# Another explicit order for the first task list of a gated attention and state-space kernel

## The chip, the cores and the metric

The kernel runs on one core of one Trainium2 chip. The metric is the device time of one execution in microseconds (us). Durations of single instructions come from a profile of one execution. A core has these engines, each with a queue of its own that is run in order: TensorE (PE; its weight loads are shown apart, as PEld), VectorE (DVE), ScalarE (ACT), GpSimd (POOL) and SyncE (SP, which here only issues transfers). They wait for each other through semaphores.

## The reference

With x of 2048 rows and 640 columns:

```python
g = sigmoid((x * gate_w).sum(-1, keepdims=True))
a = attention(x, wqkv) @ wo        # 32 heads of 20; each row looks at itself and 7 rows before it, 2 apart
b = conv(x, K) + x * Dskip         # per column, over the rows, through an FFT of length 4096
return g * a + (1 - g) * b
```

The convolution's kernel K has 2048 taps for each of the 640 columns and is made from parameters: with dt = exp(log_dt), K[d, l] is the real part of the sum over 192 states n of C[d, n] * dt * B[d, n] * exp(dt * A[d, n] * l), all complex.

## The kernel before

The work is written down as *tasks*. `Plan.add` records a name, the engines that could run it, nominal durations, a function that emits its instructions, and what it depends on. A task that may run on ScalarE or on VectorE (an eviction out of PSUM, a scaling) has both letters, "A" and "D". `Plan.order` then reads a list of numbers: number k is the k-th task recorded, and a letter behind it (97A, 99D) says which engine runs it. `Plan.emit` emits the tasks in that order and ties each instruction to the one before it on its engine, so that the list alone sets the order of every engine's queue, SyncE's and GpSimd's transfers included. There are two lists. SEQ1 has 1090 tasks and covers all up to the transforms; SEQ2 has 237, covers the spectral products, the inverse transform and the output, and starts when SEQ1's work is done.

The tasks of SEQ1, by name, with the lines that their instructions have in the profile:

- Parameters (L564 to L616): 74 tasks, most on VectorE and ScalarE, turn the parameter arrays into twelve pieces, stored to DRAM (sp0 to sp11). The lin tasks (L597, L599) are those of them that may run on either engine.
- turn0 to 9 with tev0 to 9 (L200, L470): x transposed. late0 to 59 (L291): the projections to q, k and v, five products each, into the PSUM tile tb; lev0 to 59 evict them (L470 on ScalarE, L472 on VectorE). lst (L317) stores v.
- gate to gst: the gate g.
- Attention, for eight blocks sc of 256 rows: prod (L351, VectorE) and lg (L357, TensorE) make the logits; max, neg, exp, sum and at the softmax; ast and asb (L396, L401, SyncE) send it to DRAM and fetch it back spread; vc (L345, GpSimd) fetches v; pv (L420, VectorE) weighs it; gat (L426) sums; oT (L470, L472) evicts; wo (L444) projects; ga (L453 on ScalarE, L455 on VectorE) scales by g and evicts; gaS (L464) stores.
- K, in ten chunks c of 64 columns: L (L721, SyncE) fetches parameters; arg (L748, TensorE) makes arguments, two in flight in the PSUM tile ar; act (L760 sine, L762 exponential, ScalarE) evaluates them, 18 to a chunk; pq (L783 to L785, VectorE) multiplies, three to a chunk; kmm (L801, TensorE) sums, four to a chunk, each of 64 weight loads and 64 products; fin (L1215, VectorE) gathers.
- After chunks 4 and 9, half of K is expanded: shift, move, near, own and other build tile X (L832 to L847); xst (L873 to L876) stores it to DRAM and xld (L881) loads it back as kc.
- First transforms (L1232), each evicted with a task of its own (L470, L472): f1 (ten, of kc's first half), fu (twenty, of x itself) and fk (ten, of kc's second half). rows (L946) fetch x for fu.

What sets the end of SEQ1 is written by hand only in so far as the list is: the second half's X, store, load, and the ten fk with their evictions are its last chain, and the attention's last blocks and the fu stand around it.

Of the kernel before, what the change touches and what calls it, by code (L numbers as in the profile page):

```python
# [63 lines left out]
105A 93A 22 24 34D 35D 31 36 39 42 108 109A 25 86 118 106 90 119A 102 107A 32 103A 87A 110 96 84 16 38 30 111A 135 45 97A 40 33 46 41 136A 98 99A 43 44 229 51D 52 47 53  # L64
60 62D 122 146 85A 123A 57 147A 91A 125 129 230 126A 61 63 112 48 130A 113A 50 231 59 64A 152 154 153A 65A 155A 67 139 222 232 66 233 49 58 69 54 140A 68 70 55 71 72 234
127 137 73 235 128A 236 143 237 138A 223 144A 516 238 133 265 239 131 134D 240 148 267 224 132A 241 242 150 225 149A 151A 226 243 266 269 517 244 563 562 245 518 520 268
141 270 519 521 271 522 524 272 523 273 994 124 221 145 228 264 156 525 274 526 528 167 275 301 168D 142A 527 529 276 530 532 531 533 178 534 536 180 535 537 179A 303 538
540 539 541 175 181D 246 176D 186 542 544 277 278 543 545 187A 279 182 546 548 302 304 157 554 305 307 547 183A 549 158A 159 184 160A 306 308 550 552 551 553 185D 309 337
173 280 609 281 608 227 177 188 310 564 566 171 311 174A 565 312 567 313 172A 161 314 568 570 162A 569 571 556 315 339 165 572 574 338 573 575 166D 341 555 340 576 577
578 342 169 343 345 579 170A 163 580 582 199 581 583 584 586 585 587 557 344 346 558 588 590 589 591 200A 249 164D 559 347 600 373 203 592 594 593 204A 595 348 210 211A  # L70
205 560 596 598 206D 375 561 349 597 207 208D 350 201 351 189 602 599 202A 190A 610 612 611 613 601 374 376 377 614 616 247 615 617 379 618 620 191 248A 619 621 622 624
378 380 197 623 192A 625 626 628 252 381 605 409 198A 627 629 603 604 630 631 632 606 633 634 635 382 636 216 212 411 383 607 637 213D 646 316 655 352 654 317 638 217A
639 640 384 250 642 641 385 251A 643 644 645 214 386 656 648 387 195 215A 657 658 660 647 253 410 412 196A 659 661 254A 701 700 388 662 664 663 665 193 194A 282 651 413
666 667 668 255 257 670 256D 218 669 671 672 673 649 674 675 285 258D 415 219D 676 677 650 678 679 414 680 681 682 259 683 684 686 685 687 652 688 689 692 417 416 209 300
690 418 702 691 703 704 261 705 260A 706 708 283 707 709 710 653 694 445 419 262A 288 711 712 693 714 713 715 284D 447 697 716 718 717 719 695 720 721 722 420 724 723 725
755 756 263 353 726 727 286 289 728 729 730 696 732 731 733 734 698 421 735 318 287D 290D 738 699 736 291 737 757 758 759 760 739 761 762 422 763 765 764 766 740 423 743
292D 741 767 768 801 802 769 446 448 742 771 293 770 773 772 775 774 776 777 744 778 294A 779 781 295 780 782 783 784 449 321 745 793 451 795 746 785 787 786 789 297 788
296A 790 791 803 792 804 805 450 806 807 794 809 808 811 298A 810 812 319 813 453 320A 814 815 796 816 817 818 452 819 820 821 454 823 822 824 825 826 798 749 324 455 481
827 828 322 456 829 797 830 831 832 457 325 747 748A 833 458 834 835 799 836 837 323D 483 839 326A 750 459 800 424 847 848 299 389 751 894 893 460 220 336 372 752 849 327
838 850 851 482 852 841 485 853 484 854 855 840 857 856 858 859 486 861 860 487 328D 489 862 842 863 329 331 865 844 330D 864 866 867 869 488 868 871 870 873 843 872 874  # L80
875 877 333 876 878 879 881 880 882 845 354 332D 885 846 887 883 884 895 897 490 896 899 898 901 886 900 903 902 905 355 334A 904 906 491 357 360 356D 890 907 908 909 910
753 940 335 939 425 888 911 912 913 915 914 916 492 917 918 919 920 358 361 921 889 923 922 359D 362D 390 924 925 891 927 926 929 363 928 930 941 942 943 365 931 364D 892
366D 933 945 944 946 932 947 367 949 948 493 368D 950 951 952 369 953 391 955 393 934 392D 396 936 954 956 370A 935 494 957 371 754 995 996 997 408 998 999 1000 444 1001
1002 958 959 394 960 961 963 397 395A 962 964 398A 937 965 967 966 968 399 1010 400A 1011A 401 969 1026 402A 970 403 971 405 495 938 977 979 404D 426 406D 429 1027A 972
973 974 1024 1025A 978 1022 1023A 980 1014 1015A 1012 427 1013A 1028 1029A 461 496 407 428D 432 975 430 976 1018 431D 1019A 982 462 1016 433 434A 981 1020 435 1017A 1021A
1032 1033A 1030 437 1031A 1036 983 1037A 436D 1034 439 1064 438D 465 984 440D 985 1035A 1042 1065A 441 986 1043A 987A 1044 1066 1045A 1067A 463 1054 442D 988 989 464D 468
# [1225 lines left out]
```

## Time and profile before

| what | us |
| --- | --- |
| median of 3 runs | 365.01 |
| lowest, highest run | 363.01, 368.32 |
| profiled execution, its own time | 360.97 |
| its span, from the first to the last instruction | 359.0 |
| mean granted TensorE clock in it | 0.961 |

A page of the profile gives each engine's busy time, and groups of instructions by line: line, engine, operation, what is written and read, the shape, the count, then busy time and mean nanoseconds of one, then the engine's idle time just before them and what ended it. A timeline shows instructions in order of time with the idle time before them in brackets. A table by stretches gives each engine's busy time between two points of the span. Back-to-back instructions of VectorE and ScalarE overlap by about 0.1 us in the records. "issue" is idle time in which the engine waited for nothing that the profile shows.

### The profile page before, as it was taken

The page shows a single profiled execution, that of the slowest core. Times are in us where ns is not written, and L with a number is a line of the kernel's source. Part 1 is how long each engine was busy: PE and PEld are TensorE (multiplying, and loading weights), DVE is VectorE, ACT ScalarE, POOL GpSimd, SP SyncE. Part 2 cuts the span into 40 slices and gives each one's busy share as a digit, 9 for nine tenths or more (in the row PEclk, how much of TensorE's full clock was granted, in tenths as well). Part 3 has the DMA queues.
Part 4 walks back from the last instruction along what each step waited for, and adds up shares of the span by engine and source line. Part 5 has one row for each costly group of instructions (what it writes and reads, how often), then busy time and mean ns, then how long its engine had stood idle before and what let it go on. Part 6 is the DMA issues. An engine that isn't in the chain of part 4 may idle for free. (4 is left out here: it accounts for less than half of the span.)

```text
span 359.0 us, 12203 instructions
## 1 busy us (share of the span) xinstructions
PE 293.7 (82%) x5271; PEld 173.4 (48%) x5286; DVE 311.5 (87%) x413; ACT 303.0 (84%) x417; POOL 78.3 (22%) x125
## 2 busy tenths in 40 slices
PE   0199999699999999888887869999997799978760
PEld 0065564234544545445443424566664556647650
DVE  2899999669999899999998987999993479999982
ACT  1699997578989999999997979999895599888881
POOL 8930090211020100100012122416010023310032
PEclk9999999989999999999998978999998899999995
DMA  7951289421501611461256867489653149943047
GB/s 259 370 175 57 82 213 268 120 66 19 150 11 27 122 40 19 140 129 30 71 109 192 190 152 137 95 177 256 172 153 101 38 126 225 228 95 75 4 98 199
DMA packets 44042, 46.60 MB, mean 130 GB/s; under 512 B 24517, under 2 KB 38133, under 8 KB 43733
## 3 DMA queue, kind: packets, MB, share of 16 engines
q1 hardware_dynamic: 36116, 24.43, 26.2%
q0 software_dynamic: 5840, 20.55, 22.5%
q10 hardware_dynamic: 2032, 0.85, 0.9%
q8 instruction: 41, 0.67, 0.8%
q14 instruction: 13, 0.10, 0.1%
HBM read 31.31 MB, written 14.51 MB: 128 GB/s over the span
## 5 line engine op out<-in xcount | busy, mean ns | idle before, releaser
L291 PE MATMUL tb<-bufA 128*128 128x512 bf16 x285 | 71.7, 387 | 2.8 <-issue 1.1
L748 PE MATMUL ar<-Rarg,L 64*128 64x304 bf16 (+1 forms) x480 | 55.3, 282 | 14.7 <-ACT big L760 5.9
L760 ACT ACTIVATE big<-ar 128x608 bf16<-128x608 int16 x96 | 59.0, 681 | 8.2 <-PE ar L748 5.7
L762 ACT ACTIVATE big<-ar 128x864 bf16<-128x864 f32 x60 | 50.3, 917 | 3.6 <-PE ar L748 3.3
L291 PEld LDWEIGHTS <-bufA 128*128 128x128 bf16 x300 | 33.2, 120 | 31.7 <-issue 9.3
L420 DVE TENSOR_TENSOR pv<-vc,asb 128x4096 bf16<-128x4096 bf16 (+1 forms) x24 | 46.3, 1928 | 1.4 <-PE tb L426 1.4
L748 PEld LDWEIGHTS <-L 64*128 64x128 bf16 x480 | 21.4, 94 | 48.8 <-issue 41.9
L1009 PEld LDWEIGHTS <-PHI 128*128 128x128 bf16 x288 | 26.8, 99 | 18.0 <-issue 8.4
L801 PE MATMUL kps<-qq,pt 128*32 128x22 bf16 (+1 forms) x2560 | 26.3, 175 | 4.2 <-issue 4.2
L444 PE MATMUL tb<-wo_sb,oT 128*128 128x320 bf16 x160 | 28.1, 311 | 0.0
L801 PEld LDWEIGHTS <-pt 128*32 128x32 bf16 (+1 forms) x2560 | 22.5, 91 | 11.6 <-issue 8.7
L351 DVE TENSOR_TENSOR prod<-qk 128x2048 bf16<-128x2048 bf16 x20 | 24.1, 1220 | 2.9 <-PE lg L357 2.8
L351 DVE TENSOR_TENSOR prod<-prj 128x2048 bf16<-128x2048 bf16 x20 | 24.0, 1219 | 0.6 <-PE lg L357 0.5
L345 POOL DMA_DIRECT2D vc<-vS x16 | 11.5, 725 | 57.1 <-DVE pv L420 54.0
L426 PE MATMUL tb<-pv,ind 128*64 128x512 bf16 (+1 forms) x192 | 22.4, 361 | 0.2
L785 DVE TENSOR_TENSOR qq<-big 128x1408 bf16<-128x1408 bf16 x24 | 21.2, 885 | 0.0
L470 ACT ACTIVATE bufA<-bp 128x1024 bf16<-128x1024 f32 x16 | 16.0, 1032 | 5.6 <-PE bp L1232 5.5
L1009 PE MATMUL fp<-big,PHI 128*128 128x320 bf16 x112 | 17.9, 304 | 3.0 <-ACT sp_u L470 3.0
L200 PE MATMUL ar<-ident,xn 128*128 128x128 bf16 x80 | 8.1, 263 | 15.0 <-DMA xn<-in_A_x_dram 14.3
L470 ACT ACTIVATE sp_u<-fp 128x1280 bf16<-128x1280 f32 x14 | 17.3, 1237 | 3.4 <-PE fp L1009 3.4
L470 ACT ACTIVATE prj<-tb 128x512 bf16<-128x512 f32 x28 | 17.1, 612 | 3.1 <-PE tb L291 3.0
L470 ACT ACTIVATE big<-bp 128x1024 bf16<-128x1024 f32 x19 | 18.6, 1023 | 1.0 <-PE bp L1232 0.8
(173 smaller groups left out, 587.2 us busy)
## 6 DMA issues: line engine op xcount, KB each, us to landing
vc<-vS POOLq DMA_DIRECT2D x16, 327.5 KB, 6.9
PHI<-c_phi POOLq DMA_DIRECT2D x8, 384.0 KB, 4.9
Sprm<-pc SPq DMA_DIRECT2D x12, 240.0 KB, 2.0
L<-Sprm SPq DMA_DIRECT2D x80, 36.0 KB, 2.6
xn<-in_A_x_dram SPq DMA_DIRECT2D x4, 640.0 KB
gaS<-ga SPq DMA_DIRECT2D x8, 320.0 KB, 3.0
Usb<-in_A_x_dram POOLq DMA_DIRECT2D x8, 320.0 KB, 5.0
gaF<-gaS SPq DMA_DIRECT2D x8, 320.0 KB, 7.3
```

The lines of the kernel that those rows point to most:

```text
L291: nc.tensor.matmul(ppf, self.wq[:, kt, which * D + e:(which + 1) * D:5], self.xT[:, c0 // 1024, kt, c0 % 1024:c0 % 1024 + SC], start=(kt = ...
L351: nc.vector.tensor_tensor(b[e][:], self.part(ch, 0)[:, e, o:o + C].unsqueeze(1).to_broadcast([128, W, C]), win(self.part(ch, 1)[:, e, :], ...
L420: nc.vector.tensor_tensor(b["pv", e][:, 0:2 * n], taps, aw, ALU.mult)
L426: nc.tensor.matmul(b["op", e][64 * a:64 * a + 64, 0:n, :], self.twin, b["pv", e][:, a:2 * n:2, w, :], start=(w == 0), stop=(w == HV - 1), ...
L444: nc.tensor.matmul(apf[:, :320], b["oT"][:, e, i * 128:(i + 1) * 128], wo_sb[:, e, hf * 320:(hf + 1) * 320], start=(e == 0), stop=(e == 4))
L470: nc.scalar.activation(o, i, ACT.Identity)
L748: nc.tensor.matmul(ar[:, g2, a0:a0 + ncol], L[rows, sb, gp, l0:l0 + 128], R[rows, c0:c0 + ncol], start=True, stop=True, tile_position=(64 ...
L760: nc.scalar.activation(dst[:, 2 * gp:2 * gp + 2, sub, :], ar[:].bitcast(I16)[:, :, 0:2 * SW:2], ACT.Sin, scale=SCL)
L762: nc.scalar.activation(dst[:, 2 * gp:2 * gp + 2].rearrange("p g s n -> p g (s n)"), ar[:, :, 0:2 * EW], ACT.Exp)
L785: nc.vector.tensor_tensor(qq[:], trg[:, :, KI:].rearrange("p a (v m) -> p a v m", v=2), exq[:, :, KI:].unsqueeze(2).to_broadcast([128, 32, ...
L801: nc.tensor.matmul(kps[32 * g:32 * g + 32, h, NM * ql:NM * ql + NM], pt[rows, k, v, :], qq[rows, k, v, :], start=(g not in started), stop= ...
L1009: nc.tensor.matmul(o.rearrange("p (c x) -> p c x", x=32), phis[fb][:, fl, kind, :], B[:, :, 2 * f1 + ri].rearrange("p c q g -> p c (q g)") ...
```

## The change

Only the text of SEQ1 changes. It has the same 1090 numbers in another order, and other letters behind 53 of them. As its description says, the order was made by exchanges in a play that gives each task a measured length of its own. The first and the last lines of both lists:

```diff
 SEQ1 = """
-0 2 3 1 6 8 4 14 13 26 5 7 27 9 10D 11D 12 18 74 76 28 75A 77A 78 79A 82 80 83D 15 17 23 81A 114 115D 120 94 56 121D 19 20 21 88 116 95A 89A 117A 37 100 92 104 101A 29
...
-1055A 497 443 990 1038 466 1004 1006 1009 1005 1008 1007 1003 480 991 993 1039A 1050 469 1062 467D 1051A 470D 1063A 498 1068 471 1040 473 1069A 1041A 472D 992 1046 1048
-475 474A 1047A 1049A 501 476A 477 1060 1056 1061A 478D 1057D 499 479 1058 1052 502 504 500A 1059A 1053A 505 503A 506D 1074 1070 507 1075A 1071D 1082 509 1080 508D 1083A
-510D 1081A 511 1088 1084 512D 1089A 1085D 513 514A 1076 1072 1077D 1073A 515 1078 1086 1079D 1087A
+8 0 2 3 6 1 7 14 4 13 5 26 27 9 28 994 10D 74 18 76 75A 11D 77A 78 12 79A 82 15 83D 80 81A 16 17 114 56 19 120 115D 20 23 90 116 121D 91A 21 104 117A 84 37 22 94 29 38 24
...
+1008 433 480 1021A 981 462 1032 431A 1003 1030 434A 1033A 435 1031A 1036 465 983 1037A 1034 437 1035A 436D 1064 984 438A 439 1065A 985 988 986 497 441 987A 1044 440A 989
+1042 1045A 463 1043D 990 991 442A 1038 464D 466 443 1039A 468 1068 467A 1066 1069A 469 1067D 1050 470D 1060 498 1051A 471 1061A 1054 992 993 473 1055A 472D 1062 474D 1040
+501 1063A 475 1041A 1046 477 1047A 476D 1048 478D 1056 499 1049D 479 1057A 500A 504 1052 1058 1053A 502 1059A 505 503D 1070 506A 1074 1071A 507 1075D 509 508D 1082 1080
+510D 511 1083D 1081A 513 512A 1088 514D 1072 1089A 515 1073D 1084 1086 1085D 1087A 1078 1076 1079D 1077A
 """.split()
```

In these lines 436, 438, 440 and 442 are ga500, ga501, ga510 and ga511, 426 to 443 are block 5 from pv to the store, 462 to 479 block 6's, 498 to 515 block 7's; 981 is pq91's second kmm, 982 and 983 are pq92 and its kmm, 984 fin9, 985 to 989 shift1, move1, near1, own1 and other1, 990 to 993 the stores and loads of kc; 1030 to 1069 are the fu with their evictions, 1070 to 1089 the fk with theirs.

The tasks that change their engine, counted by kind:

| kind | from ScalarE to VectorE | from VectorE to ScalarE |
| --- | --- | --- |
| lin | 1 | 1 |
| lev | 23, 27, 31, 40, 44, 46, 52, 55 | 19, 41, 43, 53, 54, 56, 59 |
| oT (block, part) | 02, 04, 20, 24, 42, 44, 72 | 14, 30, 50, 52, 62, 74 |
| ga (block, row half, column half) | 010, 101, 401, 601, 610, 711 | 001, 100, 200, 210, 501, 510, 511, 710 |
| evictions of fu and fk | fu 6, 9, 18; fk 1, 2, 6 | fu 13; fk 0, 3 |

Transfers are reordered too. On SyncE's queue, for one, the part from chunk 2's loads on was L20, ast2, L31, ast3, L30, asb2, L41, L40, ast4, L50, L51 and is L20, L30, L31, ast2, asb2, L41, L40, L51, L50, ast4, ast3; and xst0S, L81, L80, ast6 became L80, xst0S, ast6, L81. On GpSimd's queue lst32 stood ahead of vc768 and vc1024 and now stands behind them.

More of the change, by code (lines that the diff above doesn't have):

```diff
@@ new lines @@
+696 419 727 698 284D 728 389 286 699 447 729 730 263 731 732 287D 289 733 738 734 420 290A 736 735 291 801 737 757 740 293 758 759 421 802 761 760 422 762 763 739 292A
+294D 423 765 764 318 295 766 767 741 768 769 742 743 770 297 446 771 321 772 773 774 775 776 777 778 779 448 793 780 744 296A 781 783 298A 319 782 449 784 785 786 787
+320D 788 789 324 790 791 450 792 803 451 353 372 804 805 325 806 745 807 848 453 220 809 808 794 810 811 746 795 812 813 814 815 452 816 817 818 819 749 820 821 822 823
```

42 lines of the change are left out of this document (19 added, 23 removed).

## The prediction

> **What bounds the kernel now.** I read the page's busy times first, then the table of busy time by stretches, because a mean over stages hides which engine is late in each. The first task list is run from the start to about 283 us of the span and the second from there on; the profiled execution took 360.97 us with a span of 359.0, so 2.0 us lie around the span.
>
> ```profile
> PE 293.7 (82%) x5271; PEld 173.4 (48%) x5286; DVE 311.5 (87%) x413; ACT 303.0 (84%) x417; POOL 78.3 (22%) x125
> ```
> ```profile
> core 0: us, PE busy (x) PEld busy (x) DVE busy (x) ACT busy (x) POOL busy (x), PEclk, DMA share, GB/s
> 62.00:85.00 23.00, 19.07 (x131) 8.05 (x132) 15.96 (x22) 16.26 (x26) 3.24 (x7) 0.93 0.30 77
> 85.00:185.00 100.00, 90.84 (x2101) 47.94 (x2108) 98.29 (x136) 94.82 (x145) 9.26 (x13) 1.00 0.32 73
> 185.00:225.00 40.00, 32.63 (x858) 16.72 (x858) 34.65 (x49) 34.57 (x51) 8.19 (x14) 0.87 0.70 163
> 225.00:265.00 40.00, 38.20 (x861) 25.17 (x851) 39.27 (x55) 38.49 (x52) 11.93 (x19) 1.00 0.69 173
> 265.00:283.30 18.30, 13.96 (x166) 9.18 (x165) 11.18 (x13) 12.47 (x15) 0.77 (x2) 0.90 0.35 108
> ```
>
> The columns are the stretch, its length, then busy time (and count) of PE, weight loads, VectorE, ScalarE, GpSimd, then the granted TensorE clock. From 85 to 185 us VectorE is busy 98.29 of 100 us, from 225 to 265 it is busy 39.27 of 40. There no order can win: only work taken off VectorE shortens it. What an order can win lies in three holes: 62 to 85 (VectorE idle 23.00 - 15.96 = 7.0 us, ScalarE 6.7), 185 to 225 (5.4 and 5.4) and 265 to 283.3 (7.1 and 5.8). So the question is what the new list does in the holes, and how much VectorE work stands ahead of whatever ends the stage.
>
> What ends it is a round trip through DRAM. VectorE finishes the second half of the expanded kernel (tile X, task other1), SyncE and GpSimd store it, then load it back as kc, and only then can the ten fk transforms start. I read it from the timelines of VectorE, SyncE and TensorE:
>
> ```profile
> 248.52 2.28 DVE L420 TENSOR_TENSOR pv<-vc,asb 128x4096 bf16<-128x4096 bf16 x1
> 250.72 1.00 DVE L455 TENSOR_SCALAR ga<-tb,g_sb 128x320 bf16<-128x320 f32 x2
> 251.64 2.28 DVE L420 TENSOR_TENSOR pv<-vc,asb 128x4096 bf16<-128x4096 bf16 x1
> 253.84 0.52 DVE L1215 CAST E<-kps 128x352 bf16<-128x352 f32 x1
> 254.28 0.54 DVE L455 TENSOR_SCALAR ga<-tb,g_sb 128x320 bf16<-128x320 f32 x1
> 254.74 0.19 DVE L832 TENSOR_TENSOR E<-E,Dk 128x80 bf16<-128x80 bf16 x1
> 254.94 0.55 DVE L455 TENSOR_SCALAR ga<-tb,g_sb 128x320 bf16<-128x320 f32 x1
> 255.41 1.66 DVE L847 COPY X<-E 128x640 bf16<-128x640 bf16 x8
> 256.99 0.73 DVE L847 COPY X<-nxt 128x80 bf16<-128x80 bf16 x3
> ...
> 270.46 0.42 DVE L472 CAST oT<-tb 128x256 bf16<-128x256 f32 x1 [0.93 <-PE tb L426]
> 274.06 1.22 DVE L472 CAST bufA<-bp 128x1024 bf16<-128x1024 f32 x1 [3.18 <-PE bp L1232]
> ```
> ```profile
> 257.34 0.37 SPq L875 DMA_DIRECT2D Kx<-X  x1
> ...
> 264.07 1.45 SPq L881 DMA_DIRECT2D kc<-Kx  x2
> ```
> ```profile
> 272.78 1.24 PE L1232 MATMUL bp<-F1c,kc 64*128 64x128 bf16 x16 [2.37 <-DMA kc<-Kx]
> ...
> 283.30 2.29 PE L1009 MATMUL fp<-bufA,PHI 128*128 128x320 bf16 x8 [1.11 <-ACT bufA L470]
> ```
>
> X is complete at 257.7, its store is issued at 257.34 to 257.8, its load at 264.07, and TensorE, idle for 2.37 us, starts on kc at 272.78; the second list's first product follows at 283.30. Between 253.84 and 257.7 VectorE has no gap at all: the end of the first list is set by how much VectorE work stands ahead of X, plus 15.1 us of transfers, plus 10.5 us for the last stage.
>
> **The change part by part.** No operation is added. Both lists have the same 1090 tasks; their order differs on every engine, and 53 evictions, scalings and shifts change between ScalarE (A) and VectorE (D). The prices, from the groups by line:
>
> ```profile
> L470 ACT ACTIVATE prj<-tb 128x512 bf16<-128x512 f32 x28 | 17.1, 612 | 3.1 <-PE tb L291 3.0
> L470 ACT ACTIVATE oT<-tb 128x512 bf16<-128x512 f32 (+1 forms) x10 | 5.6, 557 | 0.6 <-PE tb L426 0.6
> L453 ACT ACTIVATE ga<-tb,g_sb 128x320 bf16<-128x320 f32 x12 | 6.4, 535 | 0.2 <-PE tb L444 0.2
> L470 ACT ACTIVATE big<-bp 128x1024 bf16<-128x1024 f32 x19 | 18.6, 1023 | 1.0 <-PE bp L1232 0.8
> L472 DVE CAST prj<-tb 128x512 bf16<-128x512 f32 x7 | 4.8, 685 | 2.2 <-ACT big L760 2.2
> L472 DVE CAST oT<-tb 128x512 bf16<-128x512 f32 (+1 forms) x14 | 8.4, 610 | 4.1 <-PE tb L426 4.0
> L455 DVE TENSOR_SCALAR ga<-tb,g_sb 128x320 bf16<-128x320 f32 x20 | 10.8, 546 | 1.9 <-PE tb L444 1.9
> L472 DVE CAST bufA<-bp 128x1024 bf16<-128x1024 f32 x4 | 4.9, 1225 | 4.0 <-PE bp L1232 4.0
> ```
>
> *The whole balance.* VectorE takes 28 tasks and gives 25: one lev more (+0.69), one oT more (+0.61), two ga fewer (-1.09), three fue or fke more (+3.67); the lin tasks cancel. That is +3.9 us on VectorE and, by the ScalarE rows, -0.61 - 0.56 + 1.07 - 3.07 = -3.2 us on ScalarE. Where these lie decides.
>
> *The hole of 62 to 85.* Ahead of the first product of the chunks (pq00) VectorE takes lev23, lev27, lev40 and lev44 and gives lev19 and lev41: 2 x 0.69 = +1.4 us. Its 7.0 us of idle time there hide that; without that cover it would be +1.4 on the end. ScalarE is 2 x 0.61 = 1.2 us lighter by the first activation of chunk 1, but idles 6.7 us in the same hole, so this gives between 0 and -1.2; I take -0.3, nearer to nothing, because TensorE is busy 19.07 of 23 there.
>
> *From 85 us to the last product pq92.* Ahead of pq92 VectorE's difference is +1.4 in all, which is the 1.4 of the hole: nothing is added or saved in the saturated stretch. ScalarE, up to the last chunk activation, is lighter by 2.3 us in all (one lev and four oT fewer, one ga more); being the less busy engine there it gives nothing of its own. I take 0, with bounds of -1.1 (what ScalarE sheds after the hole) and +1.1.
>
> *Between pq92 and X.* Before, VectorE runs pv60, ga500, ga501, pv62, fin9, ga510, shift1, ga511, own1, other1; after, pv60, pv62, ga500, fin9, shift1, own1, other1. Three scalings leave the path. Each holds VectorE for 0.46 to 0.47 us from start to start (254.28 to 254.74, 254.94 to 255.41): 3 x 0.47 = -1.4 us. TensorE loses wo501 ahead of the last kmm, so it is not later. What could be late next is near1 on ScalarE; it gains ga501 (0.54) and loses fue6 (1.02) ahead of it, so it isn't.
>
> *From X to the end.* The transfers are the same, 15.1 us. Behind X, VectorE takes three fue (6, 18, 9) for one (13), and ga601, ga610 and oT72 for oT62 and oT74: 2 x 1.23 + 2 x 0.55 - 0.61 = about +3.0 us before the first fk eviction. The cover is its idle 3.18 us ahead of 274.06 and 0.93 ahead of 270.46. It covers by about 1 us; with that cover gone each further us is on the end. In the last stage VectorE now has five fk casts of 1.23 where it had four, ScalarE five of 1.02 where it had six; both idle there, so the price lies between 0 and 1.2, and I take +0.2.
>
> The sum is -0.3 + 0 - 1.4 + 0.2 = -1.5 us: from the profiled 360.97 to 359.5, and from the median of 365.01 (its runs go from 363.01 to 368.32, the profiled one lying below all three) to 363.5.
>
> [...]
>
> **The rivals.** *Faster by over 2%: the hole of 185 to 225 closes.* Two of its stalls are TensorE standing still inside one run of equal products, with nothing to wait for:
>
> ```profile
> 187.88 0.63 PE L801 MATMUL kps<-qq,pt 128*32 128x22 bf16 x61
> 190.22 0.19 PE L801 MATMUL kps<-qq,pt 128*32 128x22 bf16 x3 [1.72 <-issue]
> ```
> ```profile
> 209.82 0.45 PE L801 MATMUL kps<-qq,pt 128*32 128x22 bf16 x39 [2.08 <-issue]
> 210.59 1.25 ACT L760 ACTIVATE big<-ar 128x608 bf16<-128x608 int16 x2 [1.92 <-issue]
> ```
> ```profile
> 251.49 0.50 PE L801 MATMUL kps<-qq,pt 128*32 128x22 bf16 x46 [0.44 <-issue]
> ```
> ```profile
> q8 instruction: 41, 0.67, 0.8%
> ```
>
> 41 transfers, 0.67 MB in all, so 16.3 KB each, for 5271 + 5286 TensorE instructions are one for 257 instructions: I read the stalls as TensorE out of instructions, its refill held up by the other transfers (DMA share 0.70 there). ScalarE's 1.92 shows that such a stall passes on almost whole. Where the runs fall among the refills changes with the order. If both stalls go (-3.8) and the other 1.6 us of that hole with them, and the hole of 62 to 85 gives its 1.2, the time is 363.5 - 3.8 - 1.6 - 0.9 = 357.2. For it: nothing ties the stalls to the work. Against: part of that hole goes with the clock of 0.87, and no row ties that to the order. I give 0.26.
>
> *Slower by over 2%: TensorE runs out of instructions more often.* A kmm task is 64 loads and 64 products, 128 instructions in 0.63 us. Two of them with nothing between use up one refill. On TensorE's queue such pairs stood twice (kmm110 and 111, 810 and 811); now five times (010 and 011, 311 and 320, 510 and 511, 710 and 711, 810 and 811). Each stall costs 1.7 to 2.1, say 1.9. From four more stalls on (+7.6) it decides; five are 363.5 + 9.5 = 373.0. Against it: the stalls of before lie at kmm520, kmm700 and (0.44) kmm920, none of them in a pair, so a pair alone doesn't make one. I give 0.17.
> [...]
>
> *Slower, but within 2%: a queue in front of the loads of L.* On SyncE's queue L30 and L31 now stand ahead of ast2 and asb2, ast3 behind ast4 and L50, and xst0S behind L80, which waits for chunk 6's last products.
>
> ```profile
> PE ar L748 <- DMA L<-Sprm: 2.7, 2, 1.7
> ```
>
> TensorE waited 2.7 us for L before; as much again gives 366.2. For it: an entry that waits on that queue holds up all behind it. Against: the first product of L's later chunks never stood long before. I give 0.12.
>
> **How the numbers follow.** The likeliest case has 0.45 and 363.5 us, its own range 360.5 to 366.5 from the bounds above. With the third rival, and the nearer parts of the other two, that makes 0.57 within 2% (357.7 to 372.3, about what a measurement of this kernel can tell from no change), 0.26 faster, 0.17 slower. The range for 8 in 10 reaches into both rivals: down to 355.0, a third of the first hole beside 357.2, and up to 371.0, four stalls.
>
> **What would show it.** VectorE's rows between the last qq and the X copies should hold one ga and two pv, no more, and X should be done about 1.5 us sooner; TensorE should still wait for kc; VectorE's gap before the first fk cast should shrink from 3.2 to under 1.5 us. The rows of kps with idle time by issue decide between the first two rivals: under 1 us for the faster, about 12 for the slower. I am wrong if TensorE no longer waits for kc, for then the work behind X, and not X, ends the stage.

## The result, and the profile after

| | before | after |
| --- | --- | --- |
| median of 20 runs each | 362.56 | 365.39 |
| lowest, highest run | 356.60, 370.88 | 361.37, 370.63 |
| profiled execution, its own time | 360.97 | 362.21 |
| its span | 359.0 | 360.3 |
| mean granted TensorE clock in it | 0.961 | 0.960 |

The ratio of after to before is 1.0135, with a 95% interval of 1.0091 to 1.0179: the changed kernel is slower, by about 4.9 us, which is within 2% but beyond the uncertainty of the measurement. A ratio here compares, of each kernel, the runs within 1.5% of its fastest, while a median is of all runs; in the experiments the two sometimes disagree, and then both are given.

The page's busy times of the changed kernel, and below them the table by stretches, with the columns and limits of the one shown for the kernel before:

```profile
PE 293.4 (81%) x5286; PEld 170.8 (47%) x5286; DVE 315.1 (87%) x416; ACT 301.8 (84%) x414; POOL 81.4 (23%) x125
```
```profile
62.00:85.00 23.00, 18.19 (x116) 7.50 (x115) 17.69 (x23) 14.38 (x23) 5.21 (x9) 0.94 0.50 106
85.00:185.00 100.00, 91.58 (x2004) 46.68 (x2006) 96.35 (x133) 94.31 (x143) 8.62 (x13) 1.00 0.33 71
185.00:225.00 40.00, 34.02 (x925) 17.73 (x924) 37.12 (x53) 36.81 (x56) 11.97 (x14) 0.87 0.62 154
225.00:265.00 40.00, 35.00 (x829) 21.56 (x828) 34.27 (x48) 33.00 (x47) 11.23 (x19) 0.91 0.70 169
265.00:283.30 18.30, 16.83 (x220) 11.90 (x217) 16.47 (x18) 14.08 (x18) 1.14 (x2) 1.00 0.46 144
```

The balance came nearly as counted on VectorE: 315.1 - 311.5 = +3.6 us (forecast +3.9). ScalarE's busy time fell by only 1.2 (303.0 to 301.8, forecast -3.2), because it counts the overlap of back-to-back instructions once; the durations of its instructions, added up, fell by 3.3. The first hole shrank, VectorE's idle time there going from 7.0 to 5.3 us. But the saturated stretches did not stay so. From 225 to 265 us VectorE was busy 39.27 of 40 and is now busy 34.27; from 85 to 185 it went from 98.29 to 96.35. To see what that means for X, take VectorE from 85 us to the end of its last copy into X (257.7 before, 261.7 after). Of three profiles the same row, third number VectorE: the kernel before, the changed kernel, and a second profile of the changed kernel (experiment after_again), where X ends at 259.5.

```profile
85.00:257.70 172.70, 154.46 (x3705) 84.76 (x3710) 165.58 (x231) 160.74 (x238) 28.37 (x44) 0.97 0.48 112
```
```profile
85.00:261.70 176.70, 157.30 (x3708) 84.06 (x3706) 164.78 (x228) 161.18 (x239) 31.14 (x44) 0.95 0.47 108
```
```profile
85.00:259.50 174.50, 156.91 (x3708) 83.65 (x3708) 164.40 (x229) 160.11 (x238) 30.54 (x44) 0.95 0.46 108
```

VectorE's work ahead of X is 0.8 and 1.2 us less, close to the 1.4 of the forecast. Its idle time is 172.70 - 165.58 = 7.1 before, 11.9 and 10.1 after: 4.8 and 3.0 us more. The idle time ate the saving, and more. What stands at the end, on VectorE, TensorE and ScalarE of the changed kernel in its first profile:

```profile
250.75 4.49 DVE L420 TENSOR_TENSOR pv<-vc,asb 128x4096 bf16<-128x4096 bf16 x2
255.16 0.54 DVE L455 TENSOR_SCALAR ga<-tb,g_sb 128x320 bf16<-128x320 f32 x1
256.21 0.53 DVE L1215 CAST E<-kps 128x352 bf16<-128x352 f32 x1 [0.51 <-PE kps L801]
256.77 0.20 DVE L832 TENSOR_TENSOR E<-E,Dk 128x80 bf16<-128x80 bf16 x1
257.00 1.67 DVE L847 COPY X<-E 128x640 bf16<-128x640 bf16 x8
260.93 0.76 DVE L847 COPY X<-nxt 128x80 bf16<-128x80 bf16 x3 [2.25 <-ACT nxt L470]
...
277.15 1.23 DVE L472 CAST bufA<-bp 128x1024 bf16<-128x1024 f32 x1 [0.38 <-PE bp L1232]
```
```profile
253.91 0.32 PE L801 MATMUL kps<-qq,pt 128*32 128x22 bf16 x23
255.65 0.46 PE L801 MATMUL kps<-qq,pt 128*32 128x22 bf16 x41 [1.43 <-issue]
256.05 0.67 PE L1232 MATMUL bp<-F1c,Usb 64*128 64x128 bf16 x8
256.65 1.51 PE L444 MATMUL tb<-wo_sb,oT 128*128 128x320 bf16 x5
258.09 0.66 PE L1232 MATMUL bp<-F1c,Usb 64*128 64x128 bf16 x8
258.69 1.26 PE L444 MATMUL tb<-wo_sb,oT 128*128 128x320 bf16 x5
259.78 0.64 PE L839 MATMUL nxp<-E,S 128*128 128x320 bf16 x4
...
276.34 0.77 PE L1232 MATMUL bp<-F1c,kc 64*128 64x128 bf16 x16
...
285.86 1.25 PE L1009 MATMUL fp<-bufA,PHI 128*128 128x320 bf16 x8 [1.14 <-ACT bufA L470]
```
```profile
260.46 0.70 ACT L470 ACTIVATE nxt<-nxp 128x320 bf16<-128x320 f32 x2 [0.64 <-PE nxp L839]
```

Read it as a chain. VectorE has only one scaling and two pv ahead of fin9, as forecast. But TensorE stops for 1.43 us in the last kmm, and the 3.4 us behind the stop are granted half clock (0.50): five products of a wo take 1.51 us there, 0.85 ahead of the stop. So fu2, wo501, fu17 and wo510, which stand ahead of move1 (L839), hold it until 259.78, though its input was there at 257.0. near1 (ScalarE) follows at 260.46, and VectorE waits 2.25 us for it. X ends 4.0 us later than before. Behind X the loss shrinks: TensorE goes into the fk products at 276.34 without a wait, 3.6 us later than before, and the second list starts at 285.86, 2.6 later. The second list itself took 1.3 us less (360.3 - 285.86 against 359.0 - 283.30), so this pair of profiles differs by less than the medians do.

The second profile has the late X without this end:

```profile
256.42 0.50 DVE L1215 CAST E<-kps 128x352 bf16<-128x352 f32 x1
...
258.78 0.72 DVE L847 COPY X<-nxt 128x80 bf16<-128x80 bf16 x3
```

There the stop in the last kmm is 0.27 us, the clock is 0.99 over the whole stretch from 225 to 265 us, and VectorE waits neither for the kmm nor for near1. X is 1.8 us late all the same, because pq92 already is: its first product starts at 249.54, where it started at 246.52 before and at 248.75 in the first profile. VectorE's longest waits in this profile are 1.17 and 1.37 us at 223 and 225 us, for the products of a wo, just behind a stop of TensorE of 1.52 us (221.6) and in the half clock after it (from 185 to 225 us the mean clock is 0.84 in this profile). The longest ahead of pq92 in the first profile, 1.39 us at 233.9, stands likewise behind a stop, of 1.98 us at 231.5.

### The profile page after: what moved, and what is told of

Same layout as the page of the kernel before. It is cut to its first block, busy times and chain, and to the rows that moved or that the text cites. A ratio compares the mean times of both kernels' runs of the same rounds, so it can differ in the third digit from the quotient of the medians.

```text
span 360.3 us, 12216 instructions
## 1 busy us (share of the span) xinstructions
PE 293.4 (81%) x5286; PEld 170.8 (47%) x5286; DVE 315.1 (87%) x416; ACT 301.8 (84%) x414; POOL 81.4 (23%) x125
## 5 line engine op out<-in xcount | busy, mean ns | idle before, releaser
L291 PE MATMUL tb<-bufA 128*128 128x512 bf16 x300 | 74.3, 386 | 6.8 <-DVE qk L472 4.1
L748 PEld LDWEIGHTS <-L 64*128 64x128 bf16 x480 | 20.6, 95 | 49.9 <-issue 46.4
L444 PE MATMUL tb<-wo_sb,oT 128*128 128x320 bf16 x160 | 28.6, 314 | 0.0
L426 PE MATMUL tb<-pv,ind 128*64 128x512 bf16 (+1 forms) x192 | 23.3, 368 | 0.1
L470 ACT ACTIVATE sp_k<-fp 128x1280 bf16<-128x1280 f32 x14 | 17.3, 1237 | 3.9 <-PE fp L1009 3.7
L1009 PE MATMUL fp<-bufA,PHI 128*128 128x320 bf16 x112 | 17.5, 298 | 3.7 <-ACT sp_k L470 2.2
L470 ACT ACTIVATE big<-bp 128x1024 bf16<-128x1024 f32 x17 | 16.6, 1023 | 3.4 <-PE bp L1232 3.1
L200 PE MATMUL ar<-ident,xn 128*128 128x128 bf16 x80 | 7.3, 252 | 14.5 <-DMA xn<-in_A_x_dram 13.9
L1042 DVE TENSOR_TENSOR ta<-sp_u,sp_k 128x1280 bf16<-128x1280 bf16 (+1 forms) x18 | 13.4, 750 | 6.0 <-ACT sp_u L470 3.9
```

Source lines behind the costliest of these rows:

```text
L291: nc.tensor.matmul(ppf, self.wq[:, kt, which * D + e:(which + 1) * D:5], self.xT[:, c0 // 1024, kt, c0 % 1024:c0 % 1024 + SC], start=(kt = ...
L426: nc.tensor.matmul(b["op", e][64 * a:64 * a + 64, 0:n, :], self.twin, b["pv", e][:, a:2 * n:2, w, :], start=(w == 0), stop=(w == HV - 1), ...
L444: nc.tensor.matmul(apf[:, :320], b["oT"][:, e, i * 128:(i + 1) * 128], wo_sb[:, e, hf * 320:(hf + 1) * 320], start=(e == 0), stop=(e == 4))
L470: nc.scalar.activation(o, i, ACT.Identity)
L748: nc.tensor.matmul(ar[:, g2, a0:a0 + ncol], L[rows, sb, gp, l0:l0 + 128], R[rows, c0:c0 + ncol], start=True, stop=True, tile_position=(64 ...
L1009: nc.tensor.matmul(o.rearrange("p (c x) -> p c x", x=32), phis[fb][:, fl, kind, :], B[:, :, 2 * f1 + ri].rearrange("p c q g -> p c (q g)") ...
```

## The experiments

Each table gives the median, the median of the kernel before in the same session, and the ratio with its interval. A theory's letter means the same throughout: A, the end of the list; B and F, TensorE out of instructions; C, the first part; D, the order or the engine balance by itself; E, light places of TensorE and half clock; G, near1; H, GpSimd's queue.

**Which part of the list.** Four lists were spliced at xst0S (task 716 of the old list) and at pq82 (875): the tasks that the old list has up to there, in the order and with the letters of one list, then the rest as the other list has them. For head_to_xst0, in short:

```diff
 SEQ1 = """
-0 2 3 1 6 8 4 14 13 26 5 7 27 9 10D 11D 12 18 74 76 28 75A 77A 78 79A 82 80 83D 15 17 23 81A 114 115D 120 94 56 121D 19 20 21 88 116 95A 89A 117A 37 100 92 104 101A 29
+8 0 2 3 6 1 7 14 4 13 5 26 27 9 28 994 10D 74 18 76 75A 11D 77A 78 12 79A 82 15 83D 80 81A 16 17 114 56 19 120 115D 20 23 90 116 121D 91A 21 104 117A 84 37 22 94 29 38 24
...
```

> The 716 tasks up to the store of the first half of X (xst0S) stand in the changed kernel's order with its letters, the other 374 in the old order with the old letters. Theory A (the loss is made at the end of the list, between pq82 and other1): no loss, within 0.5 us of the kernel before. Theory B (TensorE's waits for instructions make it): the changed order had 0.69 and 0.99 us of them in this part, so +0.5 to +1.7 us, and behind the cut the instructions have the same numbers as before, so nothing more. Theory C (the first part is worse: other0 was 1.8 us late): +1.8 us or more.

> The 875 tasks up to pq82 in the changed order with its letters, the rest in the old order. Theory A: the changed kernel reached pq82 2.5 us earlier than the old one, and that gain is kept with the old end: -1 to -2.5 us. Theory B: the changed order's waits for instructions in this part add up to 4.5 us against 3.8 before: between -1 and +1 us. Theory C: +1.8 us or more.

> The 875 tasks up to pq82 in the old order, the rest in the changed order with its letters. Theory A: the whole loss and more, +4 to +6 us, with VectorE's copies of X waiting for near1 on ScalarE for about 2 us. Theory B: only what the waits for instructions inside f15 and kmm920 cost, +1 to +2 us. Theory C: within 1 us of the kernel before.

> The 716 tasks up to xst0S in the old order, the other 374 in the changed order. Theory A: +4 to +5 us, the same as with the changed order from pq82 on, less the 2.5 us gained up to pq82: so +2 to +5. Theory B: +3 to +4 us (waits of 0.88, 1.98, 0.57 and 1.43 against 2.08 and 0.44 before). Theory C: within 1 us of the kernel before.

| changed order | median | before | ratio |
| --- | --- | --- | --- |
| up to xst0S | 363.11 | 360.94 | 1.0145 (1.0069 to 1.0220) |
| up to pq82 | 364.17 | 360.94 | 1.0126 (1.0037 to 1.0215) |
| from pq82 on | 363.43 | 360.94 | 1.0119 (1.0040 to 1.0198) |
| from xst0S on | 367.41 | 360.94 | 1.0233 (1.0153 to 1.0313) |

None of A, B and C holds. Each part alone costs over 1%, and the whole (1.0135) costs no more than one part. A loss that belongs to operations would add up. The parts cut at xst0S would add up to 3.8%, well above the whole; those cut at pq82 to 2.5%, which the intervals don't set apart from it. A spliced list is also a new order of its own. The loss looks like something that any other order has, and that the old order happens to lack; this is a guess from four splices.

**TensorE out of instructions.** The waits "by issue" in the rows of kps, for the kernel before, the changed one and its second profile:

```profile
L801 PE MATMUL kps<-qq,pt 128*32 128x22 bf16 (+1 forms) x2560 | 26.3, 175 | 4.2 <-issue 4.2
```
```profile
L801 PE MATMUL kps<-qq,pt 128*32 128x22 bf16 (+1 forms) x2560 | 26.8, 176 | 6.2 <-issue 6.2
```
```profile
L801 PE MATMUL kps<-qq,pt 128*32 128x22 bf16 (+1 forms) x2560 | 26.5, 176 | 5.0 <-issue 5.0
```

Counted along TensorE's queue, its longer stops of this kind come at instructions 5314, 6082 and 8130 before, and at 3778, 4290, 6594, 7106, 7874 and 8130 after. All these numbers leave 194 when divided by 256. So in these two traces the places where TensorE runs dry are fixed by the count of instructions ahead of them. The traces also hold the transfers: on the queue q8, of the kind instruction, 41 packets of 16384 bytes in each, for 5286 weight loads and 5286 products, so one for 258 instructions; I count one for each block of 256. Over the 20 profiles there are 64 stops of 0.3 us or more at such places between 75 and 286 us, and in every one of them TensorE goes on 1.2 to 1.8 us after such a packet has ended. That shows what it waited for.

How fast the block ahead of such a place is used up matters: between 75 and 286 us the old order uses up three blocks in under about 4.0 us, the shortest in 3.7 (stops taken out); the changed order seven, the shortest in about 2.3. Over all profiles about 28 of 31 blocks used up in under 3 us ended in such a stop, 13 of 38 of 3 to 4 us, and 22 of 179 of 4 to 6 us. But it isn't all: the old order's longest stop (2.08 us) stands behind a block of about 5.6 us. Its packet started 4.85 us after the place before; where no stop followed, the median was 1.0. What holds a packet back was not tested. The longest stop of the changed kernel is in the second of two adjacent kmm:

```profile
228.58 0.96 PE L801 MATMUL kps<-qq,pt 64*32 64x22 bf16 x96
231.53 0.37 PE L801 MATMUL kps<-qq,pt 64*32 64x22 bf16 x32 [1.98 <-issue]
```

Two kinds of experiment followed. One moves the places, by small products at the start that turn0 overwrites; N is 96, 64 or 128, with two instructions each (after_pad192; before_pad128 and before_pad256):

```diff
+                for i in range(N if hf == 0 and kt == 0 else 0):
+                    nc.tensor.matmul(tx[0:32, 0, 0:16], self.xn[:, 0, 0:32], self.ident[:, 0:16], start=True, stop=True)
                 for i in range(8):
```

> The changed kernel with 96 small products (192 TensorE instructions) ahead of the first turn, overwritten by it, so that every later instruction has a number higher by 192. Theory B: the waits for instructions leave kmm811 and kmm920's middle and show up inside other kmm tasks (511, 610, 700, 711, 720, 910, 911 or the end of 920), and the time moves by 3 us or more, more likely up. Rival D: the same time as the changed kernel within 0.5%, for TensorE is idle when the 96 run.

> The kernel before with 64 small products (128 TensorE instructions) ahead of the first turn, overwritten by it. Theory F (the old order is the faster one because its borders between blocks of 256 TensorE instructions fall well): in its trace, only three blocks between 75 and 286 us are used up in under 4.0 us, the shortest in 3.7; shifted by 128 there are six, of 1.5 to 3.8 us, ending at 123, 159, 166, 179, 233 and 241 us. So waits for instructions there, and +3 to +8 us against the kernel before, as slow as the changed kernel or slower. Rival D (the changed order is slower by itself): within 1 us of the kernel before.

> The kernel before with 128 small products (256 TensorE instructions) ahead of the first turn, overwritten by it: a whole block, so every later instruction keeps its place in its block. Theory F: within 1 us of the kernel before, with the waits again inside kmm520 and kmm700. Rival (the padding itself costs time, by its work or by one refill more): as slow as with 128 instructions of padding, +4 us or more.

The other thins each kmm to 76 instructions (before_lean, after_lean); the half v = 0 of its sums is left out:

```diff
-                        for v in range(2):
+                        for v in range(1, 2):
...
                                     started.add(g)
+                    for i in range(6):
+                        nc.tensor.matmul(kps[:, 0, 176:256], pt[:, 0:2].rearrange("p a v k -> p (a v k)"), pt[:, 2:4].rearrange("p a v k -> p (a v k)")[:, 0:80],
+                                         start=False, stop=False, skip_group_check=True)
```

> The kernel before, with every kmm issuing 32 of its 64 products (the half v = 0 of the sums is left out) and six longer products into unused columns, so that a kmm is 76 instructions on TensorE where it was 128, in about the same time. Theory B (TensorE's waits for instructions, and the half clock that follows each, make the differences): the waits of 1.72 and 2.08 us go, and with them the half-clock windows at 190.7 and 211.2 us: -4 to -9 us against the kernel before, mean clock over 0.97, idle time of kps by issue under 1 us. Rival D (these waits lie beside other work): within 1.5 us of the kernel before.

> The changed kernel with the same thinned kmm (half v = 0 left out). Theory B: without the waits the changed order shows the gain that was forecast for it: 1 to 2.6 us below the thinned kernel before, so -5 to -11 us against the kernel before. Rival D (the changed order or its engine balance is worse by itself): about 4 to 5 us above the thinned kernel before.

> The changed kernel once more, to see both kernels' granted clock on one chip. Theory B: +1.0 to +1.8%, with a mean clock near 0.950 against 0.966 for the kernel before, and the wait for instructions again inside kmm811 and kmm920, since the instructions have the same numbers. Rival D: +1.0 to +1.8% with the same clock in both.

| kernel | median | before | ratio | mean clock |
| --- | --- | --- | --- | --- |
| after_again | 364.97 | 360.89 | 1.0137 (1.0057 to 1.0217) | 0.952 |
| after_pad192 | 380.48 | 360.89 | 1.0440 (1.0348 to 1.0532) | 0.923 |
| before_pad128 | 368.08 | 361.99 | 1.0115 (1.0042 to 1.0189) | 0.951 (five runs) |
| before_pad256 | 363.52 | 361.95 | none | 0.958 |
| before_lean | 358.11 | 360.89 | 0.9907 (0.9856 to 0.9959) | 0.973 |
| after_lean | 363.55 | 360.89 | 1.0112 (1.0064 to 1.0160) | 0.948 |

The old order's advantage does seem to hang on where the blocks of 256 end: half a block of padding makes it as slow as the changed kernel or slower (1.0115, median +6.1 us). One of its six runs, the profiled one, took 384.15 us at a clock of 0.827 (the mean clock is of the other five); this profile has stops at three of the six places that F named (3.67, 0.55 and 0.60 us), and one of 3.05 us at another. A whole block costs 1.6 us in the median, between the two expectations and nearer to F; the stop in kmm520 is there again (1.85 us), the one in kmm700 is not. With six runs of 356 to 368 us it excludes little. The changed kernel, run again, had its stop in kmm811 again (1.55 us), in kmm920 only 0.27, and a mean clock of 0.952 beside 0.962 for the kernel before in that session. In it, 192 instructions of padding make the stops in kmm longer by far:

```profile
L803 PE MATMUL kps<-qq,pt 128*32 128x22 bf16 (+1 forms) x2560 | 27.5, 176 | 14.9 <-issue 14.9
```

Nine lie in kmm tasks (111, 320, 411, 511, 610, 711, 720, 910, 920), six of these named beforehand, three in other tasks, and all at numbers that leave 194. The median rises by (380.48 - 364.97) / (14.9 - 5.0) = 1.6 us for each microsecond of stop in kmm (the stops from one profile of each, that of after_pad192 being of its slowest run, 387.27 us): by this a stop costs more than itself. The 96 products themselves cost little: they take 2.73 us, and the first chunk's last product ends 0.9 us later than in after_again.

Thinning takes the stops out of kmm (its row has 0.0 us of idle time in both). It gives the old order 2.8 us in the median, less than B's 4 to 9. But the changed order gains only 1.4 us, and the distance between the two grows, from 4.1 us to 5.4. So B, in the form that these stops alone separate the kernels, fell. As a test it is weaker than it looks: the thinned pair has a wait that the full kernels don't have, for the rows of fu (shown below), so it doesn't say what the stops cost in the full kernels.

**Half clock.** In the clock's records half clock comes in steps of 3.41 us: it lasts 3.41 or 6.83 us in the kernel before and 3.41 or 10.24 in the changed one, the last record of each (10.08 and 10.75) aside. The same steps for the rows of TensorE: first the kernel before, two pairs of steps around its stops at 190 and 210 us, then the changed kernel around 231.5 us (second number TensorE busy, then, three from the end, the clock):

```profile
187.26:190.67 3.41, 1.49 (x81) 1.13 (x77) 2.59 (x7) 2.12 (x5) 0.65 (x1) 1.00 0.54 178
190.67:194.08 3.41, 3.41 (x27) 1.06 (x21) 2.94 (x5) 2.72 (x4) 0.00 (x0) 0.51 0.83 257
207.74:211.15 3.41, 1.33 (x50) 0.83 (x51) 3.05 (x4) 1.49 (x3) 0.00 (x0) 1.00 0.82 208
211.15:214.56 3.41, 3.03 (x80) 1.09 (x74) 2.62 (x4) 2.87 (x6) 1.11 (x3) 0.51 0.48 113
```
```profile
228.79:232.20 3.41, 1.43 (x128) 1.16 (x113) 3.41 (x5) 1.83 (x3) 1.36 (x2) 1.00 0.46 154
232.20:235.61 3.41, 3.31 (x80) 1.28 (x77) 1.07 (x3) 2.02 (x4) 0.18 (x1) 0.51 0.78 174
```

At these three stops, of 1.72, 2.08 and 1.98 us, TensorE is busy for 1.33 to 1.49 us of the step, and the next step is granted 0.51. That is one way in which a stop costs more than itself. Over the steps at full clock of 19 profiles (all but that of before_pad128), 35 of 36 with TensorE busy under 45% were followed by half clock, 54 of 139 between 45% and 70%, and 3 of 1521 above; a sharp border is not shown. Across the 105 runs of the kernel before in these sessions the mean clock goes from 0.942 to 0.978, and the time falls by 0.8 us for each microsecond of clock regained; this is a correlation, and doesn't say which is the cause.

The changed order also has light steps that hold no stop of half a microsecond or more and are followed by half clock: at 198 us in the first profile, at 178 and 199 in the second. The one at 198 and the step behind it:

```profile
198.06:201.47 3.41, 2.25 (x18) 0.78 (x17) 3.41 (x3) 3.41 (x7) 0.81 (x1) 1.00 0.40 68
201.47:204.88 3.41, 3.01 (x78) 1.53 (x76) 3.41 (x5) 3.41 (x7) 0.41 (x1) 0.51 0.73 187
```

To fill them, the sine arguments of chunks 5 to 8 were made wider, with the same number of instructions, in both orders, thinned and not:

```diff
-                                        nc.tensor.matmul(ar[:, g2, a0:a0 + ncol], L[rows, sb, gp, l0:l0 + 128], R[rows, c0:c0 + ncol],
+                                        w = 512 if kind == 0 and 5 <= c <= 8 else ncol
+                                        nc.tensor.matmul(ar[:, g2, a0:a0 + w], L[rows, sb, gp, l0:l0 + 128], R[rows, c0:c0 + w],
```

> The changed kernel with wider products in the sine arguments of chunks 5 to 8 (512 columns where 304 are used; the rest is not read), so that TensorE does more in the stretch from 160 to 220 us with the same number of instructions. Theory E (in the changed order TensorE falls below about two thirds of 3.4 us at 168, 178 and 198 us, its clock is then halved, and at half clock it is the bound): less lost clock than the changed kernel (mean clock 0.957 or more against 0.951) and 1 to 3 us less time, +0.4 to +1.1% against the kernel before, by more TensorE work. Rival D (the order or the engine balance needs the time by itself): no faster than the changed kernel, +1.3% or more, since work was added.

> The kernel before with the same wider products. Theory E: its low points (187, 208) are waits inside kmm, which the wider products do not fill: the same as the kernel before within 1.5 us. Rival D: slower by the added work, up to 2 us.

> The kernel before with the thinned kmm (half v = 0 left out) and the wider products. Theory E: it had no low point left between 85 and 240 us, so it stays at -1% (358 us) within 1 us. Rival D: slower than that by up to 2 us.

> The changed kernel with the thinned kmm (half v = 0 left out) and the wider products. Theory E: with both causes of low points taken away the distance of 5.4 us between the two thinned kernels shrinks by at least half: 361 us or less, mean clock 0.96 or more. Rival D: the distance stays at 5 us, 363.5 or more.

| kernel | median | before | ratio | mean clock |
| --- | --- | --- | --- | --- |
| before_wide | 361.11 | 363.41 | 0.9974 (0.9919 to 1.0029) | 0.971 |
| after_wide | 365.18 | 363.41 | 1.0109 (1.0045 to 1.0172) | 0.963 |
| before_lean_wide | 358.38 | 363.41 | 0.9983 (0.9938 to 1.0027) | 0.973 |
| after_lean_wide | 361.98 | 363.41 | 0.9997 (0.9946 to 1.0047) | 0.966 |

The clock rose as E said, from 0.952 to 0.963 and from 0.948 to 0.966 in the changed order. The time did not follow as E said: after_wide stands 4.1 us above before_wide, as far as the changed kernel above the old one, and the thinned pair is 3.6 us apart in the median where it was 5.4 (by the ratios, almost level; the two measures disagree). Beside the kernel before of their session, the wider products left both orders 2.3 us better in the median (before_wide -2.3; after_wide +1.8, where after_again was +4.1). So half clock at those light places is not what sets the changed kernel apart from the old one.

**The end: near1, and GpSimd's queue.** after_tail moves one thing, TensorE's move1 and ScalarE's near1, ahead of the fu and wo that stood before them (names for numbers):

```diff
-kmm920 fue3A fu2 wo501 fue2A ga500D fu17 fin9 ga501A wo510 fue17A shift1 own1 move1 asb7 wo511 near1A
+kmm920 fue3A fu2 ga500D fin9 shift1 wo501 move1 fue2A near1A fu17 ga501A wo510 fue17A own1 asb7 wo511
```

after_lean_vc puts vc1536 ahead of rows6 in the thinned changed kernel; after_lean_tail_vc has both; after_lean_wide_tail_vc has the wider arguments too.

> The changed kernel with move1 right behind wo501 (ahead of fu17 and wo510) and near1 right behind fue2 (ahead of ga501 and fue17). Theory G (the X copies wait for near1, which is late behind move1): the wait of other1 goes, 1 to 2 us less than the changed kernel, so +0.5 to +1.1% against the kernel before. Rival: the wait was half clock's doing in one profile, and the time stays at +1.35%.

> The changed kernel with the thinned kmm (half v = 0 left out), and vc1536 ahead of rows6 in GpSimd's queue. Theory H (behind the waits for instructions stands GpSimd's queue: vc1536, behind the paced rows6, comes 4 to 10 us late for pv60): no wait at pv60, 3 to 5 us less than the changed kernel with thinned kmm, so 359 to 360.5 us, and a mean clock of 0.960 or more. Rival D: 363.5 us as before.

> The same with move1 and near1 earlier too (half v = 0 left out). Theories G and H together: 358 us or less, level with the thinned kernel before (358.1) or below it by up to 1.5 us, which is the gain forecast for the order. Rival D: still 3 us or more above the thinned kernel before.

> The changed kernel with the thinned kmm (half v = 0 left out), the wider sine arguments of chunks 5 to 8, move1 and near1 earlier, and vc1536 ahead of rows6. If the four causes are all there is: mean clock 0.965 or more and 357 to 359.5 us, level with the old order thinned and widened (358.4). Rival D (the order itself needs the time): 361.5 us or more, 3 us above it.

| kernel | median | before | ratio |
| --- | --- | --- | --- |
| after_tail | 362.74 | 361.99 | 1.0074 (1.0036 to 1.0111) |
| after_lean_vc | 363.71 | 361.99 | 1.0008 (0.9961 to 1.0055) |
| after_lean_tail_vc | 364.62 | 361.99 | 1.0128 (1.0081 to 1.0176) |
| after_lean_wide_tail_vc | 363.53 | 361.95 | none |

G's forecast of the time came true: after_tail is 0.75 us above the kernel before in the median, where the changed kernel was 2.8 and 4.1 above it, and its ratio of 1.0074 lies inside the 1.005 to 1.011 expected. The last copies into X follow without a wait, although TensorE still stops in kmm920:

```profile
255.13 0.53 DVE L1215 CAST E<-kps 128x352 bf16<-128x352 f32 x1 [1.00 <-PE kps L801]
255.69 0.20 DVE L832 TENSOR_TENSOR E<-E,Dk 128x80 bf16<-128x80 bf16 x1
255.92 1.68 DVE L847 COPY X<-E 128x640 bf16<-128x640 bf16 x8
257.52 0.73 DVE L847 COPY X<-nxt 128x80 bf16<-128x80 bf16 x3
```

The intervals of 1.0074 and 1.0135 overlap by a little, so it is likely, not certain, that the order of these few tasks costs about 2 us. That VectorE's wait for near1 is the way is shown for single runs only. The wait comes with a long stop in the last kmm: 2.25, 2.40, 2.15 and 2.18 us in the profiles of after, of both lists with the changed tail and of after_pad192 (stops of 1.43 to 3.07 us), but 0.00 and 0.14 in those of after_again and after_wide (0.27 and 0.79). With the new places of move1 and near1 it is 0.00 behind a stop of 1.98; but there the clock behind the stop stayed full (all products of wo together take 27.5 us in it, 28.6 in the changed kernel's first profile), so this one profile doesn't show the new places at half clock.

H's forecasts failed (359 to 360.5 us, then 358 or less), and what vc1536 is worth is not settled: by the ratio it gives the thinned kernel 1%, by the median nothing, or 0.9 us beside the kernel before of its session, and with the tail added it is slower again. The kernel with all four changes came out at 363.53 where 357 to 359.5 was expected if the four causes were all; the rival had 361.5 or more. Its profile, of a run of 366.37 us, shows what stands in the way. It reaches pq92 at 243.2 us, 2.4 us ahead of before_lean_wide, and then TensorE stands inside the first product of a fu (first fence), which needs the rows that GpSimd fetches one after the other (second fence, its copies that wait for each fetch). That these rows are what TensorE waits for there is read from the two queues; in after_lean the same wait has its transfer named. Third and fourth fence, after_lean and before_lean:

```profile
244.82 0.29 PE L1236 MATMUL bp<-F1c,Usb 64*128 64x128 bf16 x1
254.62 1.06 PE L1236 MATMUL bp<-F1c,Usb 64*128 64x128 bf16 x15 [9.51 <-issue]
```
```profile
232.44 0.18 POOL L949 COPY pace<-Usb 32x2 bf16<-32x2 bf16 x1 [3.64 <-DMA Usb<-in_A_x_dram]
...
237.27 2.76 POOL L949 COPY pace<-Usb 32x2 bf16<-32x2 bf16 x1 [2.50 <-DMA Usb<-in_A_x_dram]
...
245.48 4.21 POOL L949 COPY pace<-Usb 32x2 bf16<-32x2 bf16 x1 [4.72 <-DMA Usb<-in_A_x_dram]
```
```profile
L1235 PE MATMUL bp<-F1c,Usb 64*128 64x128 bf16 x160 | 10.3, 258 | 12.4 <-DMA Usb<-in_A_x_dram 11.9 <-ACT big L470 0.3
```
```profile
L1235 PE MATMUL bp<-F1c,Usb 64*128 64x128 bf16 x160 | 10.3, 254 | 2.6 <-issue 2.1 <-ACT big L470 0.3
```

In both orders the last kmm stands behind fu1, fu0 and fu3 on TensorE's queue. So what is gained up to pq92 cannot reach X before the rows have landed. The wait differs from run to run: in the five profiles of thinned changed kernels the row has 0.6, 2.3, 6.9, 10.0 and 12.4 us of idle time, and these runs took 359.33, 362.94, 362.70, 366.37 and 372.68 us; in the two of the thinned old order 0.6 and 2.6. In before and after the row has 0.5 us: there it is no part of the result. Of the lists that compute everything, none beat the kernel before beyond the uncertainty; before_wide (0.9919 to 1.0029) is level with it.

## Why the prediction was wrong

*X about 1.5 us sooner.* Wrong: 4.0 us later in the first profile, 1.8 in the second. The term that was worked out held roughly: three scalings left VectorE's path, forecast -1.4, measured -0.8 and -1.2 of work between 85 us and X.

*"I take 0, with bounds of -1.1 (what ScalarE sheds after the hole) and +1.1", for the stretch from 85 us to pq92.* This is the step that failed. It took an engine that is busy 98 of 100 us for one whose idle time can't grow, and so summed work alone. pq92 came 2.2 us later in the first profile and 3.0 in the second (246.5 to 248.7 and 249.5), by waits. Ahead of X VectorE's idle time grew by 4.8 and 3.0 us. That one order keeps VectorE full doesn't say that another with the same work does. The longest of these waits stand behind TensorE's stops for instructions; that the stops make up the whole of it is not shown.

*"What could be late next is near1 on ScalarE; it gains ga501 (0.54) and loses fue6 (1.02) ahead of it, so it isn't."* Wrong in the first profile, by 2.25 us, right in the second, where VectorE didn't wait for near1. The work ahead of near1 on its own engine was counted, but not what feeds it, move1 on TensorE behind fu and wo. In the old list VectorE came to fin9 at 253.84, 1.9 us after the last kmm had ended (251.49 + 0.50), and had ga510 and ga511 to do behind it: that covered TensorE's work ahead of move1. This work is three fu and two wo before, two and two after: move1 starts 2.9 us after the kmm's end before, 2.4 in the second profile, and 3.7 at half clock in the first. With the three scalings gone the cover is thin: it is enough when TensorE doesn't stop (fin9 started 1.4 us after the kmm in the second profile), and not when it stops (0.51 us of waiting at fin9 in the first). The price of the order there, by after_tail, is likely about 2 us; the profiles do not show it in every run.

*The rival "TensorE runs out of instructions more often".* The mechanism was the right one to name: the stops in kmm went from 4.2 to 6.2 and 5.0 us. Its test was wrong. Adjacent pairs of kmm were counted, but of the six stops only two lie in the five pairs (kmm320 and kmm811); they come at fixed numbers, where the 256 instructions ahead were used up before the next packet was there. Its size was off too: 1 to 2 us more, not 7.6. Whether these 1 to 2 us, with the half clock behind them, make up the rest of the loss stays open: with the stops taken out of both orders the distance did not shrink, but the thinned changed kernels wait for rows instead.

*The rival of the closed hole, and the queue in front of the L loads.* Of the first, the two stops of 1.72 and 2.08 us did vanish from the hole of 185 to 225 (VectorE's idle time there fell from 5.4 to 2.9), and others came at 220.5, in the same hole, and at 231.5 and 255.7. Of the second nothing was seen: in both profiles of the changed kernel TensorE's weight loads of L wait less for its transfers, 1.3 and 1.0 us where it was 3.6.

*From X to the end.* The cover held: VectorE's gap before its first cast of fk is 0.38 us, forecast under 1.5. That TensorE no longer waits for kc is the sign that was given for being wrong, and it showed in the first profile (in the second it waits 1.0 us). Here it took no time: the fk started 3.6 us later than before, X ended 4.0 later.

*Size.* -1.5 us was forecast, with 355 to 371 as the range; 365.39 lies inside, but the way was wrong: the gain of 1.5 us was a loss of 2.8 in the median. A range that wide would have held either.

## What to carry to other kernels

A saturated engine is not a guarantee: when a whole order changes, its idle time must be forecast wait by wait, and for each thing that leaves a path the next one must be followed through every engine that feeds it. In a kernel with runs of short products like this one, count TensorE's instructions to each border of 256, where these stops lay, and look at how long the block ahead of it lasts. Here stops followed about 28 of 31 blocks of under 3 us and 13 of 38 of 3 to 4, but also one of about 5.6, so a long block is no safety. Moving such borders changed the time by as much as this change did (a ratio of 1.0115 for half a block ahead of the old order, beside 1.0135). Where an old order happens to lie well at these borders, a new one can lose that even though its sum is better. And take a second profile before naming a wait: the clearest one of the first, near1, was not in the second.

## What was not expected of the hardware

- TensorE's stops for instructions come at queue numbers that leave 194 when divided by 256, with padding and without, and end 1.2 to 1.8 us after a packet of 16384 bytes on the queue of the kind instruction (64 stops in 20 profiles).
- A light step of TensorE (under 45% of 3.41 us busy) was followed by half clock in 35 of 36 cases, though TensorE had worked for 1.3 to 1.5 us in some of them.
- 96 tiny products at the start, which delay the first chunk by 0.9 us, made the kernel 15.5 us slower in the median.
- A copy of 32x2 elements on GpSimd, 0.18 us at its shortest, took 2.76 and 4.21 us between row fetches in the profile of after_lean_wide_tail_vc, 3.75 in that of after_lean and 3.27 in the changed kernel's first; why is not shown.
